# The second product's 256-column products moved into one column group, pieces of three thirds moved out of it

## The chip, the cores and the metric

The kernel runs on one core of a Trainium2 chip. The metric is the device time of one execution in microseconds. TensorE (PE in the profile) does the matrix products, VectorE (DVE), ScalarE (ACT) and GpSimd (POOL) the elementwise work, and SyncE (SP) and POOL issue the transfers. Matrix products are summed up in PSUM, which has eight banks of 512 float32 columns over 128 partitions.

## The reference

`x` is (8, 4096, 192), `weight` (8, 7), `w_in` (192, 2048), `w_out` (2048, 192), all float32.

```python
w = softmax(weight, axis=-1)                       # 7 taps for each of 8 heads
attn = causal depthwise convolution of x over the sequence with w
x = attn.reshape(32768, 192)
h = x @ w_in                                       # 32768 x 2048
g = h * np.clip(h + 3.0, 0.0, 6.0) / 6.0
return (g @ w_out).astype(np.float32)              # 32768 x 192
```

## The kernel before, in words

The 32768 tokens are worked on in 32 blocks of 1024. A block has a first layer (convolution, the product with `w_in`, and the hardswish) and a second layer (the product with `w_out`). Block 0 has a second layer of its own (`out_direct`), blocks 1 to 30 use the steady form of `second_layer`, and block 31 a variant of it for the end (`last`). This text is about the 30 steady blocks.

**First layer** (`first_layer`, matmuls on L512). Sixteen units go through four pairs of PSUM banks. When a unit's products are done, ACT applies a relu (L303), DVE multiplies (the gate, L307), and the pair of banks is free again. The second layer takes three of the four pairs for its banks `x_`, `b`, `y_`, `c`, `a`, and its two banks `f` and `h` are the fourth pair, `free_slots[0]`, which is the one that the last unit of the first layer has used.

**Second layer** (`second_layer`). The product with `w_out` is done by Strassen-like formulas: seven products, numbered 1 to 7, of sums of quarters of g and of w_out, each 96 output columns wide (three thirds of 32). The output of PE is cut into four column groups of 32, numbered 0 to 3 here, which write the PSUM partitions 0-31, 32-63, 64-95 and 96-127 (`first`, `second`, `third`, `fourth`). The groups work at the same time, so that four products of 32 output columns go on side by side. All of their matmuls are recorded on one line, L640.

A *plain* product of one third takes eight matmuls of 512 columns, two slots each (`plain`, `put(j, 2, ...)`). Products 1, 2, 4 and 5 have one third that is done by a second level of the same formulas: seven small products of four matmuls of 256 columns, one slot each (`small`, `level_two`), between which ACT copies intermediate results from one place of PSUM to another (`steps`: small product 1 goes to A, A is copied to B, 6 is added to B, B is copied to C, and so on). A float32 matmul runs as two passes.

The order is written out by hand. Each of the four groups has its own list and a clock in slots, and every list must end at 80. All other work of the stage (ACT copies, DVE sums, transfers, stores) is put in with `do(t, fn)`, at slot t - 0.5. At the end all events are sorted by slot and issued in that order, so that each engine gets its instructions in the order of those times. There is no planner, and no wait is written by hand: the framework puts in a semaphore wait where an instruction touches what an earlier one on another engine still uses.

```python
        def do(t, fn, *args, **kw):
            streams[3].append((t - 0.5, lambda: fn(*args, **kw)))
...
        events = sorted(((t, fn) for st in streams for t, fn in st), key=lambda x: x[0])
```

Before, product 2's small products are spread over the groups: 1, 7, 2 and 4 in group 0, 5 in group 1, 3 in group 2, 6 in group 3, with copies between them at fixed slots (20, 31.9, 39.6, 40, 44, 64, 64.4). The level two of product 1 is in group 1, of 4 in group 2 and of 5 in group 3. Group 0 has 16 matmuls of 256 columns, the others 32 each.

Of the kernel before, what the change touches and what calls it, by code (L numbers as in the profile page):

```python
# [25 lines left out]
def kernel(  # L26
# [16 lines left out]
    N = 512  # L43
    G = 2
    TB = G * N
    D2 = P // 2
# [41 lines left out]
    for base, dma in ((0, nc.scalar), (D2, nc.sync)):  # L88
        dma.dma_start(
            out=w_sb[base : base + D2],  # L90
            in_=weight.unsqueeze(1).to_broadcast([H, GJ, KC]),
# [126 lines left out]
    for n in range(AHEAD):  # L218
# [8 lines left out]
        out=e_sb[:], in0=w_sb[:], in1=mx[:].to_broadcast([P, KC]), op=ALU.subtract  # L227
# [54 lines left out]
    def take():  # L282
        return free_banks.pop(0)
# [72 lines left out]
    every = range(NP)  # L356
# [90 lines left out]
    def rows(q):  # L447
        return slice(q * QS, (q + 1) * QS)
# [9 lines left out]
    def add(out, x, y, op=ALU.add):  # L458
        nc.vector.tensor_tensor(out=out, in0=x, in1=y, op=op)  # L459
# [112 lines left out]
    halves = slice(0, TH), slice(TH, N)  # L572

    def four_parts(x):
        return [x[:, c::2, t] for t in halves for c in range(2)]
# [14 lines left out]
    def quarters(w):  # L590
        return [
            w_out[:, c::2, w, q * QS : (q + 1) * QS] for c in range(2) for q in range(2)
        ]
# [12 lines left out]
    def second_layer(i, between):  # L606
        last = i + 1 == NB
        ours = [free_slots.pop(0) for _ in range(3)]
        x_, b, y_, c, a, _ = (psum[:, 2 * n + k] for n in ours for k in range(2))
# [3 lines left out]
        copy = nc.scalar.copy  # L613
        m = slice(0, DH)
        lo, hi = halves
        both = nc.sync, nc.scalar
        first, second, third, fourth = (rows(q) for q in range(4))
        f, h = (psum[:, 2 * free_slots[0] + k] for k in range(2))
        end = h
        V = a[fourth]  # L620
        chains = {
            j: [bank[rows(j), t] for bank in (x_, y_) for t in halves] for j in (1, 2, 3)
        }
        A2, E2, C2, D2 = f[first, lo], f[second, hi], h[first, lo], h[third, hi]
        B2 = h[second if last else fourth, hi]
        j1 = 3 if last else 1
        late = {}

# [3 lines left out]
        def put(j, cost, fn):  # L632
            streams[j].append((clock[j], fn))
            clock[j] += cost

        def do(t, fn, *args, **kw):
            streams[3].append((t - 0.5, lambda: fn(*args, **kw)))

        def matmul(j, out, w, x, start):
            nc.tensor.matmul(  # L640
                out=out, lhsT=w, rhs=x, start=start, stop=True,
                tile_position=(0, j * QS), skip_group_check=True,
            )

        def plain(j, bank, n, q, chunks, start=False):
            x, w = prod[n]
            x = S3 if x is None else x
            for k, ch in enumerate(chunks):
                put(j, 2, lambda ch=ch, k=k: matmul(
                    j, bank[rows(j)], w_out[:, ch, w, q * QS : (q + 1) * QS], x[:, ch],  # L650
                    start and k == 0,
                ))
# [8 lines left out]
        def small(n, m_, out, start=False, j=3):  # L661

            x, w = prod[n]
            sums, ws = {
                1: (shared, w_s[:, 0]), 5: (s5, w_s[:, 1]), 2: (sums2, w_s[:, 2]),
                4: (sums4[0], w_s[:, 3]),
            }[n]
            x11, x12, x21, x22 = four_parts(x)
            z1, z2, z3, z4 = four_parts(sums)
            b11, t3, b21, b22 = quarters(w)  # L670
            t1, t2, t4 = (ws[:, k] for k in range(3))
            xm, wm = {
                1: (x11, b11), 2: (x12, b21), 3: (z4, b22), 4: (x22, t4),
                5: (z1, t1), 6: (z2, t2), 7: (z3, t3),
            }[m_]
            for u in range(NP // 2):
                put(j, 1, lambda u=u: matmul(
                    j, out, wm[:, u], xm[:, u], start and u == 0
                ))
# [16 lines left out]
        def fold(p, m136):  # L696
            add(p[second, hi], p[second, hi], p[second, lo])
            add(p[second, lo], m136, p[second, lo])
# [11 lines left out]
        def p2(r, t):  # L710
            return late["p2"][r, t]

        def p3(q):
            if last:
                plain_by_halves(q, 3, q, 0)
                plain_by_halves(q, 3, q, 1)
            else:
                plain(q, b, 3, q, in_fours)
# [6 lines left out]
        p4 = Fourth()  # L725

        def level_two(n, p, order, j=3):
            A, E, B, C = chains[j]
            steps = {
                1: lambda: copy(out=B, in_=A),  # L730
                2: lambda: copy(out=p()[first, lo], in_=A),
                6: lambda: copy(out=C, in_=B),
                5: lambda: copy(out=p()[second, lo], in_=E),
                7: lambda: copy(out=p()[second, hi], in_=C),
                3: lambda: copy(out=p()[first, hi], in_=C),
            }
            to = {1: A, 2: A, 6: B, 5: E, 7: C, 3: B, 4: C}
            for k in order:
                small(n, k, to[k], k in (1, 5), j)
                if k != 4:  # L740
                    late_by = {(1, 2): 8.1, (4, 2): 8.2 if last else 19.3}.get((n, k), 0.02 if n == 4 else 0)
                    do(clock[j] + late_by, steps[k])

        rest = 6, 2, 7, 5, 4, 3
        chunks, first_fill = list(every), [True]

        def fill(k):
            plain(3, a, 5, 2, [chunks.pop(0) for _ in range(k)], first_fill.pop() if first_fill else False)
# [2 lines left out]
            for ch in every[2:6]:  # L751
                by_half(3, (a, c)[t], 2, 2, ch, t)

        plain(0, b, 4, 2, every, True)
        small(2, 1, A2, True, 0)
        plain(0, c, 7, 0, every, True)
        small(2, 7, C2, False, 0)
        small(2, 2, A2, False, 0)
        plain(0, b, 6, 0, every)
        small(2, 4, C2, False, 0)  # L760
        p3(0)

        if last:
            plain(1, b, 1, 2, every, True)
            plain(1, c, 7, 1, every[:4], True)
            plain(1, a, 2, 2, every[:2], True)
            small(2, 6, B2, False, 1)
            plain(1, c, 7, 1, every[4:])
            small(2, 5, E2, True, 1)
            plain(1, b, 6, 1, every)  # L770
            plain(1, a, 2, 2, every[6:])
        else:
            level_two(1, lambda: p1, (1,), 1)
            plain(1, c, 7, 1, every[:4], True)
            level_two(1, lambda: p1, rest, 1)
            plain(1, c, 7, 1, every[4:])
            plain(1, b, 6, 1, every)
            small(2, 5, E2, True, 1)
        p3(1)

        level_two(4, lambda: p4, (1,), 2)
# [2 lines left out]
        level_two(4, lambda: p4, rest, 2)  # L784
        plain(2, c, 7, 2, every[ahead:])
        plain(2, b, 6, 2, every)
        small(2, 3, D2, False, 2)
        p3(2)

        if last:  # L790
            level_two(1, lambda: p1, (1,))
            fill(2)
            level_two(1, lambda: p1, rest)
            fill(4)
        else:
            plain(3, b, 1, 2, every, True)
            plain(3, c, 2, 2, every[:6], True)
            small(2, 6, B2, False)
            plain(3, c, 2, 2, every[6:])
            fill(4)  # L800
        level_two(5, lambda: late["p5"], (1,))
        fill(2)
        level_two(5, lambda: late["p5"], rest)
# [5 lines left out]
        assert clock == [80] * 4  # L809

        for t in halves:
            do(30 if t == hi else 29, copy, out=p4[third, t], in_=b[first, t])
        do(25.5, copy, out=p1[third], in_=b[second if last else fourth])
        do(20, copy, out=B2, in_=A2)
        do(31.9, copy, out=C2, in_=B2)
        do(39.6, copy, out=D2, in_=B2)
        do(40, lambda: copy(out=p2(second, hi), in_=C2))
        do(44, lambda: copy(out=p2(first, lo), in_=A2))
        do(44 if last else 64, lambda: copy(out=p2(second, lo), in_=E2))

        for t, job in between:
            do(t, job)
# [31 lines left out]
        if last:  # L854
            do(49, lambda: copy(out=late["p5"][third], in_=V))
        else:
            do(56.6, lambda: copy(out=p2(third, slice(0, N)), in_=c[fourth]))
        do(64.4, lambda: copy(out=p2(first, hi), in_=C2))
        if last:
            do(64.4, lambda: add(p2(third, slice(0, N)), a[second], p1[third]))  # L860
            for bank, t in ((a, lo), (c, hi)):
                do(64.4, lambda bank=bank, t=t: copy(out=bank[fourth, t], in_=p2(third, t)))
        do(64.4, lambda: fold(late["p2"], D2))
        whole = slice(0, 2 * QS if last else DH)
        do(64.6, lambda: add(late["p2"][whole], late["p2"][whole], p1[whole]))
        if last:
# [92 lines left out]
    with tc.manual_schedule():  # L959
# [4 lines left out]
            out=c_sb[:], in0=e_sb[:], in1=sm[:].to_broadcast([P, KC]), op=ALU.mult  # L964
# [14 lines left out]
        b = take()  # L979
        for cols in (N, N, N // 2):  # L980

            nc.tensor.matmul(  # L982
                out=psum[:, b, 0:cols], lhsT=zeros[:, 0:P], rhs=zeros[:, 0:cols],
# [59 lines left out]
        n = 3  # L1043
        for slot, (c, group) in enumerate(parts):
            first = slot < len(early)
# [27 lines left out]
        late = ctx.enter_context(tc.tile_pool(name="late", bufs=1, reuse_waits="tile"))  # L1073
# [60 lines left out]
        last = ctx.enter_context(tc.tile_pool(name="last", bufs=1, reuse_waits="tile"))  # L1134
# [55 lines left out]
```

## Time and profile before

| | |
|---|---|
| median of 3 runs | 2195.59 us (2195.41 to 2196.65) |
| the profiled execution's own time | 2195.6 us |
| its span | 2193.8 us |
| PE busy | 2188.3 us |
| DVE busy | 1953.5 us |
| ACT busy | 1230.1 us |
| POOL busy | 1178.8 us |
| matmuls of the second layer on `g` with `w_out` (L640) | 5960 of 512 and 256 columns, mean 503 ns |
| granted TensorE clock | 1.000 |

Busy time is the time in which an engine has at least one instruction at work; matmuls of different column groups overlap, so PE counts once for up to four. "PEld" is the load of weights into PE, which goes on beside matmuls. A row of the timeline gives the start in us, how long, the engine, the line, the operation, output and input tile, their shapes, and in square brackets the idle time before it and who ended it. The chain is read backwards from the last instruction; its shares say which engine's work set the time.

### The profile page before, as it was taken

The page shows a single profiled execution, that of the slowest core. Times are in us where ns is not written, and L with a number is a line of the kernel's source. Part 1 is how long each engine was busy: PE and PEld are TensorE (multiplying, and loading weights), DVE is VectorE, ACT ScalarE, POOL GpSimd, SP SyncE. Part 2 cuts the span into 40 slices and gives each one's busy share as a digit, 9 for nine tenths or more (in the row PEclk, how much of TensorE's full clock was granted, in tenths as well). Part 3 has the DMA queues.
Part 4 walks back from the last instruction along what each step waited for, and adds up shares of the span by engine and source line. Part 5 has one row for each costly group of instructions (what it writes and reads, how often), then busy time and mean ns, then how long its engine had stood idle before and what let it go on. Part 6 is the DMA issues. An engine that isn't in the chain of part 4 may idle for free.

```text
span 2193.8 us, 53991 instructions
## 1 busy us (share of the span) xinstructions
PE 2188.3 (100%) x22984; PEld 1501.9 (68%) x22984; DVE 1953.5 (89%) x1956; ACT 1230.1 (56%) x1800; POOL 1178.8 (54%) x1028
## 2 busy tenths in 40 slices
PE   9999999999999999999999999999999999999999
PEld 4467776677766677766777667776667776677766
DVE  8888998898998889988899888999888998899977
ACT  7355565554555655555546555455565555554654
POOL 2456654565544666445655456554456554565544
PEclk9999999999999999999999999999999999999999
DMA  6277778777778777797777878777877778777776
GB/s 159 60 138 146 147 147 151 141 146 145 148 139 157 141 139 146 147 159 131 147 147 145 148 145 145 145 146 145 159 135 139 147 148 154 135 147 144 135 143 112
DMA packets 352434, 312.59 MB, mean 142 GB/s; under 512 B 211904, under 2 KB 264640, under 8 KB 352192
## 3 DMA queue, kind: packets, MB, share of 16 engines
q0 software_dynamic: 114640, 233.87, 59.3%
q1 hardware_dynamic: 235624, 74.66, 16.9%
q8 instruction: 180, 2.95, 0.6%
q10 hardware_dynamic: 1928, 0.59, 0.1%
q14 instruction: 62, 0.51, 0.1%
HBM read 31.72 MB, written 25.17 MB: 26 GB/s over the span
## 4 chain that ended last, share of the span: by engine, by line
PE 100%; DVE 0%; issue 0%
PE psum L640 49%; PE psum L512 46%; PE psum L297 2%; PE psum L342 2%; PE psum L974 0%; PE psum L982 0%; PE psum L895 0%; DVE zeros L111 0%; DVE shared L922 0%; DVE x L96 0%; DVE half L233 0%; DVE bias_e L150 0%; DVE bias_e L149 0%
## 5 line engine op out<-in xcount | busy, mean ns | idle before, releaser
L640 PE MATMUL psum<-g,w_out 128*32 128x512 f32 (+1 forms) x5960 | 922.8, 503 | 0.0
L303 ACT ACTIVATE g<-psum,half 128x1024 f32<-128x1024 f32 (+1 forms) x528 | 574.4, 1092 | 485.6 <-PE psum L512 485.6
L307 DVE SCALAR_TENSOR_TENSOR g<-g,psum 128x1024 f32<-128x1024 f32 (+1 forms) x528 | 608.2, 1180 | 106.4 <-ACT g L303 106.1
L640 PE MATMUL psum<-s,w_out 128*32 128x512 f32 (+1 forms) x3024 | 657.9, 585 | 0.0
L640 PEld LDWEIGHTS psum<-g,w_out 128*32 128x32 f32 x5960 | 375.0, 110 | 248.9 <-issue 116.0
L512 PE MATMUL psum<-y_own,w_in 64*128 64x512 f32 x4464 | 515.1, 388 | 0.0
L512 PE MATMUL psum<-y_other,w_in 64*128 64x512 f32 x4464 | 510.9, 386 | 0.0
L512 PEld LDWEIGHTS psum<-y_own,w_in 64*128 64x128 f32 x4464 | 415.8, 184 | 112.1 <-issue 26.0
L512 PEld LDWEIGHTS psum<-y_other,w_in 64*128 64x128 f32 x4464 | 418.1, 184 | 87.8
L588 POOL TENSOR_TENSOR shared<-g,shared 128x256 f32<-128x256 f32 x248 | 358.0, 1444 | 54.8 <-DVE g L307 29.0
L1080 DVE SCALAR_TENSOR_TENSOR y<-x,c_sb,y 128x1536 f32<-128x1536 f32 x186 | 334.7, 1799 | 0.2
L554 POOL DMA_DIRECT2D s<-g x123 | 147.1, 1198 | 266.4 <-PE psum L640 123.5
L640 PE MATMUL psum<-g,w_s 128*32 128x256 f32 x1488 | 282.3, 379 | 0.0
L640 PEld LDWEIGHTS psum<-s,w_out 128*32 128x32 f32 x3024 | 197.2, 110 | 74.0 <-issue 16.0
L554 POOL DMA_DIRECT2D g<-g x124 | 180.8, 1519 | 106.7 <-DVE s L415 106.7
L640 PE MATMUL psum<-z,w_s 128*32 128x256 f32 x992 | 228.1, 379 | 0.0
L640 PE MATMUL psum<-z,w_out 128*32 128x256 f32 x992 | 227.2, 379 | 0.0
L459 DVE TENSOR_TENSOR g<-g 128x1024 f32<-128x1024 f32 x124 | 148.7, 1220 | 44.5 <-PE psum L640 44.5
L588 POOL TENSOR_TENSOR shared<-g 128x256 f32<-128x256 f32 x124 | 92.0, 742 | 171.4 <-DVE g L307 171.4
L640 PEld LDWEIGHTS psum<-g,w_s 128*32 128x32 f32 x1488 | 138.0, 110 | 42.7
L266 POOL DMA_DIRECT2D y_other<-y_own x90 | 48.0, 534 | 213.2 <-DVE shared L459 213.1
L554 POOL DMA_DIRECT2D z<-g x62 | 95.8, 1545 | 116.3 <-ACT z L557 116.3
(118 smaller groups left out, 2706.4 us busy)
## 6 DMA issues: line engine op xcount, KB each, us to landing
y_other<-y_own POOLq DMA_DIRECT2D x180, 384.0 KB, 8.1
g<-g POOLq DMA_DIRECT2D x124, 512.0 KB, 6.0
s<-g POOLq DMA_DIRECT2D x123, 512.0 KB, 6.4
z<-g POOLq DMA_DIRECT2D x62, 512.0 KB, 7.2
out_dram<-shared SPq DMA_DIRECT2D x376, 64.0 KB, 3.9
x<-in_x_dram SPq DMA_DIRECT2D x53, 388.5 KB, 5.7
z<-g SPq DMA_DIRECT2D x31, 512.0 KB, 3.3
stage<-in_moe_w_in_dram SPq DMA_DIRECT2D x16, 192.0 KB, 5.0
```

What stands on the lines that cost most here:

```text
L266: dma.dma_start(out=to[D2:P], in_=part[0:D2])
L297: nc.tensor.matmul(out=psum[:, b], lhsT=w[r], rhs=src, start=start, stop=stop, skip_group_check=onto,)
L303: nc.scalar.activation(r6, h, ACT.Relu, bias=half[:], scale=1.0 / 6.0)
L307: nc.vector.scalar_tensor_tensor(out=g_, in0=g_, scalar=1.0, in1=h, op0=ALU.min, op1=ALU.mult)
L342: lambda p=p: nc.tensor.matmul(out=bank[j * QS : (j + 1) * QS, tokens], lhsT=w_out[:, p, w, cols], rhs=x[:, p, tokens], start=(first and p ...
L459: nc.vector.tensor_tensor(out=out, in0=x, in1=y, op=op)
L512: nc.tensor.matmul(out=psum[:, 2 * slots[n] + k], lhsT=r32(w_in_parts[part][r, c, s]), rhs=r32(y_other[0][r, part, s] if group else y_own[ ...
L554: nc.gpsimd.dma_start(out=out, in_=x, accum_op=ALU.add)
L588: engine.tensor_tensor(out=o, in0=p, in1=q, op=op)
L640: nc.tensor.matmul(out=out, lhsT=w, rhs=x, start=start, stop=True, tile_position=(0, j * QS), skip_group_check=True,)
L1080: jobs.append(lambda k=k: nc.vector.scalar_tensor_tensor(out=y[:], in0=x[:, :, k : k + N], scalar=c_sb[:, k : k + 1], in1=y[:], op0=ALU.mu ...
```

## The change

It changes steady blocks alone (`last` keeps the old order).

- All seven small products of product 2 are now in group 0, through `level_two(2, ..., 0)`, with the places A, E in bank `f` and B, C in bank `h`, partitions `first`. Small product 1 moves from slot 16 to slot 4, right behind the first two chunks of plain product 4.
- The other six chunks of that plain third of product 4 go to group 3 (slots 16 to 28, into `a[fourth]`). What group 0 has summed up so far is copied there by ACT: `a[fourth] <- b[first]`, due at 4.2. `p4[third]` is then read from `a[fourth]`.
- Two chunks of the plain third of product 5 go from group 3 to group 1 (slots 60 to 64, into `a[second]`): ACT copies `a[second] <- a[fourth]` at 52.1 and back at 64.5.
- The last two chunks of the plain third of product 2 go from group 3 to group 2 (slots 60 to 64, into `a[third]`): ACT copies `a[third] <- c[fourth]` at 48.1, and `p2[third]` is read from `a[third]` at 64.4.
- The seven copies that joined product 2's scattered small products are gone. Each group now has 28 matmuls of 256 columns. The number of matmuls is the same.

In the changed kernel the second layer's matmuls are on L641, the six copies of level two on L731 to L736, the relu and the gate still on L303 and L307.

```diff
+        chains[0] = [bank[first, t] for bank in (f, h) for t in halves]
...
+                        (1, 2): 8.1, (4, 2): 8.2 if last else 19.3, (2, 2): 8, (2, 7): -0.05, (2, 5): 4,
...
-        plain(0, b, 4, 2, every, True)
-        small(2, 1, A2, True, 0)
-        plain(0, c, 7, 0, every, True)
-        small(2, 7, C2, False, 0)
-        small(2, 2, A2, False, 0)
-        plain(0, b, 6, 0, every)
-        small(2, 4, C2, False, 0)
...
+        else:
+            plain(0, b, 4, 2, every[:2], True)
+            level_two(2, lambda: late["p2"], (1,), 0)
+            plain(0, c, 7, 0, every, True)
+            level_two(2, lambda: late["p2"], rest[:5], 0)
+            plain(0, b, 6, 0, every)
+            level_two(2, lambda: late["p2"], rest[5:], 0)
         p3(0)
...
-            small(2, 5, E2, True, 1)
+            plain(1, a, 5, 2, every[4:6])
...
-        small(2, 3, D2, False, 2)
...
+            plain(2, a, 2, 2, every[6:])
...
             plain(3, b, 1, 2, every, True)
+            plain(3, a, 4, 2, every[2:])
             plain(3, c, 2, 2, every[:6], True)
-            small(2, 6, B2, False)
-            plain(3, c, 2, 2, every[6:])
-            fill(4)
+            fill(2)
+            chunks[2:4] = []
...
+            do(4.2, copy, out=a[fourth], in_=b[first])
+            do(48.1, copy, out=a[third], in_=c[fourth])
+            do(52.1, copy, out=a[second], in_=a[fourth])
+            do(64.5, copy, out=a[fourth], in_=a[second])
...
-            do(56.6, lambda: copy(out=p2(third, slice(0, N)), in_=c[fourth]))
+            do(64.4, lambda: copy(out=p2(third, slice(0, N)), in_=a[third]))
```

More of the change, by code (lines that the diff above doesn't have):

```diff
@@ L623, in second_layer @@
         }
+        chains[0] = [bank[first, t] for bank in (f, h) for t in halves]
         A2, E2, C2, D2 = f[first, lo], f[second, hi], h[first, lo], h[third, hi]
-        B2 = h[second if last else fourth, hi]
+        B2 = h[second, hi]
         j1 = 3 if last else 1
@@ L740, in level_two @@
                 if k != 4:
-                    late_by = {(1, 2): 8.1, (4, 2): 8.2 if last else 19.3}.get((n, k), 0.02 if n == 4 else 0)
+                    late_by = {
+                        (1, 2): 8.1, (4, 2): 8.2 if last else 19.3, (2, 2): 8, (2, 7): -0.05, (2, 5): 4,
+                    }.get((n, k), 0.02 if n == 4 else 0)
                     do(clock[j] + late_by, steps[k])
@@ L752, in last_third @@
                 by_half(3, (a, c)[t], 2, 2, ch, t)
-        plain(0, b, 4, 2, every, True)
-        small(2, 1, A2, True, 0)
-        plain(0, c, 7, 0, every, True)
-        small(2, 7, C2, False, 0)
-        small(2, 2, A2, False, 0)
-        plain(0, b, 6, 0, every)
-        small(2, 4, C2, False, 0)
+        if last:
+            plain(0, b, 4, 2, every, True)
+            small(2, 1, A2, True, 0)
+            plain(0, c, 7, 0, every, True)
+            small(2, 7, C2, False, 0)
+            small(2, 2, A2, False, 0)
+            plain(0, b, 6, 0, every)
+            small(2, 4, C2, False, 0)
+        else:
+            plain(0, b, 4, 2, every[:2], True)
+            level_two(2, lambda: late["p2"], (1,), 0)
+            plain(0, c, 7, 0, every, True)
+            level_two(2, lambda: late["p2"], rest[:5], 0)
+            plain(0, b, 6, 0, every)
+            level_two(2, lambda: late["p2"], rest[5:], 0)
         p3(0)
@@ L786, in second_layer @@
         plain(2, b, 6, 2, every)
-        small(2, 3, D2, False, 2)
+        if last:
+            small(2, 3, D2, False, 2)
+        else:
+            plain(2, a, 2, 2, every[6:])
         p3(2)
@@ L811, in second_layer @@
         for t in halves:
-            do(30 if t == hi else 29, copy, out=p4[third, t], in_=b[first, t])
+            do(30 if t == hi else 29, copy, out=p4[third, t], in_=(b[first, t] if last else a[fourth, t]))
         do(25.5, copy, out=p1[third], in_=b[second if last else fourth])
[L814 to L819, printed above, removed]
+        if last:
+            do(20, copy, out=B2, in_=A2)
+            do(31.9, copy, out=C2, in_=B2)
+            do(39.6, copy, out=D2, in_=B2)
+            do(40, lambda: copy(out=p2(second, hi), in_=C2))
+            do(44, lambda: copy(out=p2(first, lo), in_=A2))
+            do(44, lambda: copy(out=p2(second, lo), in_=E2))
+        else:
+            do(4.2, copy, out=a[fourth], in_=b[first])
+            do(48.1, copy, out=a[third], in_=c[fourth])
+            do(52.1, copy, out=a[second], in_=a[fourth])
+            do(64.5, copy, out=a[fourth], in_=a[second])
         for t, job in between:
@@ L856, in second_layer @@
         else:
-            do(56.6, lambda: copy(out=p2(third, slice(0, N)), in_=c[fourth]))
-        do(64.4, lambda: copy(out=p2(first, hi), in_=C2))
+            do(64.4, lambda: copy(out=p2(third, slice(0, N)), in_=a[third]))
+        if last:
+            do(64.4, lambda: copy(out=p2(first, hi), in_=C2))
         if last:
@@ L862, in second_layer @@
                 do(64.4, lambda bank=bank, t=t: copy(out=bank[fourth, t], in_=p2(third, t)))
-        do(64.4, lambda: fold(late["p2"], D2))
+        do(64.4, lambda: fold(late["p2"], D2 if last else chains[0][2]))
         whole = slice(0, 2 * QS if last else DH)
```

## The prediction

> **What bounds the kernel now.** I read the page's busy shares first, then the chain that ended last in order of time, then one steady block of the timeline, engine by engine, and last the compiled program of the changed kernel, which says what each matmul waits for.
>
> ```profile
> PE 2188.3 (100%) x22984; PEld 1501.9 (68%) x22984; DVE 1953.5 (89%) x1956; ACT 1230.1 (56%) x1800; POOL 1178.8 (54%) x1028
> ...
> PE 100%; DVE 0%; issue 0%
> PE psum L640 49%; PE psum L512 46%; PE psum L297 2%; PE psum L342 2%; PE psum L974 0%; PE psum L982 0%; PE psum L895 0%; DVE zeros L111 0%; DVE shared L922 0%; DVE x L96 0%; DVE half L233 0%; DVE bias_e L150 0%; DVE bias_e L149 0%
> ```
>
> What matters here is the 100% of PE, and that the chain never leaves it.
>
> ```profile
> 468.53 34.55 PE psum L640 x291
> 503.08 32.86 PE psum L512 x288
> ```
>
> PE never stands still: a steady block is 34.55 us of second layer (L640, the stage that the change edits) and 32.86 us of first layer (L512), and the 30 steady blocks repeat these two numbers. Asked who PE waits for from 99 us to 2190 us, the trace names nobody. So only two things can move the time: the number and length of the passes in the longest column group, and a wait that PE does not have today. In the stage that starts at 468.46 these rows carry the prices:
>
> ```profile
> 467.69 0.84 PE L512 MATMUL psum<-y_other,w_in 64*128 64x512 f32 x6
> 468.46 2.33 PE L640 MATMUL psum<-g,w_out 128*32 128x512 f32 x25
> 470.22 0.59 PE L640 MATMUL psum<-s,w_out 128*32 128x512 f32 x1
> ...
> 490.84 0.38 PE L640 MATMUL psum<-g,w_s 128*32 128x256 f32 x1
> ...
> 491.49 0.38 PE L640 MATMUL psum<-g,w_s 128*32 128x256 f32 x1
> ```
>
> ```profile
> 468.57 1.11 ACT L303 ACTIVATE g<-psum,half 128x1024 f32<-128x1024 f32 x1 [0.92 <-PE psum L512]
> 470.49 0.71 ACT L730 COPY psum<-psum 32x256 f32<-32x256 f32 x2 [0.80 <-PE psum L640]
> 475.63 0.71 ACT L732 COPY psum<-psum 32x256 f32<-32x256 f32 x2 [4.44 <-PE psum L640]
> ...
> 489.46 0.34 ACT L730 COPY psum<-psum 32x256 f32<-32x256 f32 x1 [0.65 <-PE psum L640]
> 489.74 1.48 ACT L477 ACTIVATE y_own<-y 128x1536 fp32r<-128x1536 f32 x1
> ```
>
> ```profile
> 469.72 1.22 DVE L307 SCALAR_TENSOR_TENSOR g<-g,psum 128x1024 f32<-128x1024 f32 x1 [0.81 <-ACT g L303]
> ```
>
> The reader is to see three places in time. Slot 4 of the 80 (a slot is a 256-column product, 0.43 us) is 470.22. The gate of the first layer's last unit, which reads the bank pair f, h, ends only at 469.72 + 1.22 = 470.94. ACT's first copies of the stage end at 470.49 + 0.71 = 471.20.
>
> **The change part by part.** *Passes.* Each product is two passes. Long passes follow each other every 0.43 us (plain products of one group start at 470.63, 471.06, 471.49), short ones every (491.49 - 490.84)/3 = 0.217 us. Groups 1 to 3 go from 24 long and 32 short products to 26 and 28, that is from 48 x 0.43 + 64 x 0.217 = 34.53 us to 52 x 0.43 + 56 x 0.217 = 34.51 us. Group 0 grows from 16 shorts to 28, to the same sum. So evening out saves 0.02 us a block, 30 x 0.02 = 0.6 us. I take it, bounds 0 and 1.2 us.
>
> *The first wait, at slot 4.* Before, group 0 first writes bank f at slot 16, about 468.46 + 16 x 0.432 = 475.4, long after the gate. Now it writes f at slot 4, and the compiled program has that short product waiting for DVE. Behind it on PE, in order, stand the slot-4 products of the other groups, so all four stop from 470.22 to 470.94. Worse, group 3's slot-4 product, into bank b, now waits for ACT: the new copy `a[fourth] <- b[first]` (due at 4.2) reads bank b, and the program keeps the two apart although they use different rows. On ACT that copy stands behind the two L730 copies that end at 471.20. Its own form, 32x512 from PSUM to PSUM, is not in the trace; a 32x512 copy out of PSUM takes 0.58 us (L637, L857), a 96x512 copy into PSUM 0.57 us, and a 32x256 copy between banks 0.34 against 0.36 us to SBUF. I take 0.57, with 0.34 (a 256-wide one) and 0.58 as ends. It runs from 471.22 to 471.79. From a release to the next engine's start is 0.04 us (ACT ends at 469.68, DVE starts at 469.72), and the first pass after a pause is longer by its unhidden weight load:
>
> ```profile
> L640 PE MATMUL psum<-g,w_out x192: 379/592/617, 468.5 to 502.5; 128*32 128x512 f32 x112, 128*32 128x256 f32 x80
> ...
> L297 PE MATMUL psum<-y_swapped,w_in x9: 589/589/693, 16.5 to 20.0; 64*128 64x512 f32 x9
> ```
>
> 617 - 592 = 0.025 us with a 32-column load, 693 - 589 = 0.104 us with a 128-column one; I take 0.03, since the load is a 32-column one here. Group 3 goes on at 471.86, so it loses 471.86 - 470.22 = 1.64 us (1.40 to 1.75). The gate's 0.72 us lies inside this and is not added. The stage ends with its latest group, and that is group 3.
>
> *The second wait, at slot 48.* Two long products before 490.84 put slot 48 at 490.84 - 4 x 0.43 = 489.12. There group 3 now adds to a[fourth], and a copy due at 48.1, `a[third] <- c[fourth]`, writes the same bank. The program has this product wait for that copy as well. On ACT it stands behind level two's first copy (L730 at 489.46, which waits for products ending at slot 48), before which nothing can start it: 489.46 + 0.34, then 0.57 from 489.82 to 490.39, then 0.07, against 489.12: 1.34 us. Part of the 0.34 us from slot to copy is the other groups' slower retirement, and after the first wait group 3 is itself the last; with 0.2 us for that it is 1.20. I take 1.27 (1.05 to 1.45).
>
> *Other waits.* At slots 20, 28 and 44 PE already depends on ACT copies. The pair L732 ends at 476.34, slot 20 is 477.10, so 0.76 us are spare. Group 3 running up to 1.64 - 0.72 = 0.9 us behind groups 1 and 2 can delay the release of those copies by as much, but it costs only the groups that are ahead. I take 0, up to 0.2 us a block.
>
> *ACT, DVE, POOL, SP.* ACT loses seven copies of 0.34 to 0.36 us (2.45 us) and gains six of them and four of 0.57 us (4.4 us), net 1.95 us a block. It is busy 20.57 of the stage's 34.55 us, and most new copies fall in its gaps (4.44 us idle before 475.63, 3.07 us before the last L735), so this costs nothing but for the two above; without that cover it would be 1.95 us. Counts and order of instructions on DVE, POOL and SP, their DMAs among them, are unchanged: whatever they issue moves with PE, and no transfer gets less time than before.
>
> *Sum.* 1.64 + 1.27 - 0.02 = 2.89 us a block, and the stage goes from 34.55 to about 37.4 us. 30 x 2.89 = 86.7 us. The profiled execution took 2195.6 us (span 2193.8 and 1.8 around it), the median is 2195.59, so the sum stands on either: 2282 us.
>
> *A rule beside it.* The conflict over banks is the program's. The Trainium skill, page "PSUM — Partial Sum Buffer", section "PSUM bank collisions raise a hardware error", says that two engines may use one bank at the same time if they are in different 32-partition quadrants. By that rule neither the copy out of b[first] nor the one into a[third] would have to hold group 3, and the sum would be the second rival's below; no run here shows it, and the compiled waits speak against it.
>
> **The rivals.** *It does what it says* (no new wait reaches PE): 2195.6 - 0.6 = 2195 us. For it speaks that no PE wait is in the trace now; against it that the gate ends 0.72 us after slot 4 whatever else happens. *Only the gate holds PE*, because group 3's two waits are met early: 0.72 + 0.07 = 0.79 us a block, 30 x 0.77 = 23 us, 2219 us. Against it: the copies stand in order behind copies that the trace shows ending at 471.20 and 489.80. *More than these two*: the waits at 20, 28 and 44 become real and the desynchronized groups retire each copy's source later, 0.6 us more a block: 2300 us. *The other side*: the groups' unevenness costs more than the pass counts say. The stage's 34.55 us against 80 slots of long passes only, 80 x 0.43 = 34.4, leaves at most 0.15 us a block, 4.5 us in all: 2191 us. It decides only if f were free at 470.22 and bank b at the same time; the row at 469.72 says no.
>
> **How the numbers follow.** Forecast 0.80; more waits 0.07; gate alone 0.06; does what it says 0.04; other side 0.03. The forecast's own bounds are (1.40 + 1.05) x 30 = 73 us and (1.75 + 1.45 + 0.2) x 30 = 102 us, 2269 to 2298. With the rival above at 2300, the range 2266 to 2301 leaves out little more than the three lower cases, 13 in 100, and some of the forecast's tail. About 0.2% (4.4 us) is what a measurement of this kernel can tell from no change: faster 0.03, same 0.04, slower 0.93.
>
> **What would show it.** In the changed kernel L641, the line of the second layer's matmuls, should take about 37.4 us a block, first layer 32.86 as before; PE should show two idle stretches, some 1.6 us after the stage's first 1.8 us (first released by DVE, then by ACT) and some 1.2 us near 22.5 us into it (by ACT); the new 32x512 copies should take 0.57 us. I am wrong if PE waits only for DVE, if the stage is near 34.5 us, or if a third place near slots 20 to 44 costs more than 0.2 us.

## The result and the profile after

The changed kernel takes 2281.24 us (median of 5 runs, 2280.97 to 2281.58), the one before 2195.92 us (5 runs): a ratio of 1.0388, 95% interval 1.0373 to 1.0403, slower. The forecast was 2282 us, within 2266 to 2301.

The first lines of the page of the changed kernel and its chain, to be held against the 100% and the unbroken chain of before:

```profile
span 2279.6 us, 54111 instructions
## 1 busy us (share of the span) xinstructions
PE 2239.5 (98%) x22984; PEld 1500.2 (66%) x22984; DVE 1955.7 (86%) x1956; ACT 1288.2 (57%) x1890; POOL 1177.0 (52%) x1028
...
PE 92%; ACT 5%; DVE 2%; issue 1%; ACTq 0%
```

PE has as many passes as before (22984), but the chain now leaves it, for ACT and DVE. Who PE waits for between 99 us and the end, where the same question had no answer before (columns: us in total, times, longest):

```profile
PE psum L641 <- ACT psum L638: 16.9, 30, 0.6
PE psum L641 <- DVE g L307: 14.0, 23, 0.6
PE psum L641 <- DVE x L81: 4.3, 7, 0.6
```

There are thirty waits for ACT and thirty (23 + 7) for the gate, one of each per steady block: L81 is a memset that ends within 0.01 us of the gate on L307, so the last two rows are one wait. L638 is the line of the copies. The list counts only the time in which no column group had a matmul at work. So what a block loses is larger, and group 3's wait for the first copy, during which the other groups still worked, is not in the list; it is read from the rows of the block below. One steady block in the chain in order of time (start, us, what):

```profile
484.44 1.22 DVE g L307
485.66 0.03 DVE s L415
485.69 0.02 issue
485.71 17.68 PE psum L641 x158
503.39 0.03 issue
503.42 0.36 ACT shared L732
503.78 0.96 ACT s L557
504.74 0.02 issue
504.76 0.36 ACT shared L734
505.12 0.58 issue
505.70 0.06 ACT psum L731
505.77 0.29 issue
506.06 0.56 ACT psum L638
506.62 0.04 issue
506.67 13.98 PE psum L641 x82
```

The same block on PE and on ACT:

```profile
483.18 1.93 PE L641 MATMUL psum<-g,w_out 128*32 128x512 f32 x24
485.71 0.40 PE L641 MATMUL psum<-g,w_out 128*32 128x256 f32 x1 [0.61 <-DVE x L81]
...
486.54 0.62 PE L641 MATMUL psum<-g,w_out 128*32 128x512 f32 x2
...
506.67 1.93 PE L641 MATMUL psum<-g,w_out 128*32 128x512 f32 x16 [0.56 <-ACT psum L638]
```

```profile
485.20 0.71 ACT L731 COPY psum<-psum 32x256 f32<-32x256 f32 x2 [0.80 <-PE psum L641]
485.94 0.55 ACT L638 COPY psum<-psum 32x512 f32<-32x512 f32 x1
...
505.70 0.34 ACT L731 COPY psum<-psum 32x256 f32<-32x256 f32 x1 [0.58 <-issue]
506.06 0.56 ACT L638 COPY psum<-psum 32x512 f32<-32x512 f32 x1
```

The stage starts at 483.18, so slot 4 is at 483.18 + 1.76 = 484.94 (470.22 - 468.46 before). The gate ends at 485.66 and group 0's small product starts at 485.71. The new copy ends at 485.94 + 0.55 = 486.49, and group 3 goes on at 486.54, 1.60 us late. Its 44 slots to slot 48 (by the starts of the passes, 40 slots in 20 long products of some 0.859 us, 4 in short ones of 0.432 us) end at 505.44, and it goes on at 506.67, 0.05 us after the copy's end: 1.23 us late. Between 505.51 and 506.67 no group starts a pass, though only group 3 waits for the copy.

Ahead of the second copy the chain runs through ACT's earlier work (L732, L557, L734). That work is not what held the copy: ACT then stood idle for 0.58 us, until L731 started at 505.70. L731 copies the result of group 3's small product that ends at slot 48, and it starts 0.26 us after 505.44. The profile names no releaser for it here; for the same copy in the kernel before it names PE (the row at 489.46).

The stage grows from 34.55 us to 37.40 us in the mean of the steady blocks, from the first matmul to the first one of the next stage; the span grows by 2279.6 - 2193.8 = 85.8 us, 2.86 us for each of the 30 blocks. Only part of this shows as idle time of PE, whose busy time grew by 2239.5 - 2188.3 = 51.2 us with the same passes: while one group waits, PE still counts as busy as long as another works.

### The profile page after: what moved, and what is told of

Its sections match the earlier page's. It is cut to its first block, busy times and chain, and to the rows that moved or that the text cites. A ratio compares the mean times of both kernels' runs of the same rounds, so it can differ in the third digit from the quotient of the medians.

```text
span 2279.6 us, 54111 instructions
## 1 busy us (share of the span) xinstructions
PE 2239.5 (98%) x22984; PEld 1500.2 (66%) x22984; DVE 1955.7 (86%) x1956; ACT 1288.2 (57%) x1890; POOL 1177.0 (52%) x1028
## 4 chain that ended last, share of the span: by engine, by line
PE 92%; ACT 5%; DVE 2%; issue 1%; ACTq 0%
PE psum L512 45%; PE psum L641 43%; PE psum L297 2%; PE psum L342 2%; DVE g L307 2%; ACT g L303 1%; ACT s L557 1%; ACT psum L638 1%; ACT shared L732 0%; ACT shared L734 0%; PE psum L995 0%; PE psum L1003 0%; ACT psum L731 0%; PE psum L916 0%; DVE zeros L111 0%
## 5 line engine op out<-in xcount | busy, mean ns | idle before, releaser
L641 PE MATMUL psum<-g,w_out 128*32 128x512 f32 (+1 forms) x5960 | 1013.9, 505 | 35.1 <-ACT psum L638 16.9
L303 ACT ACTIVATE g<-psum,half 128x1024 f32<-128x1024 f32 (+1 forms) x528 | 574.2, 1092 | 488.0 <-PE psum L512 472.3
L307 DVE SCALAR_TENSOR_TENSOR g<-g,psum 128x1024 f32<-128x1024 f32 (+1 forms) x528 | 608.1, 1180 | 108.9 <-ACT g L303 108.7
L641 PEld LDWEIGHTS psum<-g,w_out 128*32 128x32 f32 x5960 | 382.9, 109 | 366.5 <-issue 86.5
L641 PE MATMUL psum<-s,w_out 128*32 128x512 f32 (+1 forms) x3024 | 616.8, 587 | 0.0
L641 PE MATMUL psum<-g,w_s 128*32 128x256 f32 x1488 | 286.9, 380 | 0.0
L641 PEld LDWEIGHTS psum<-g,w_s 128*32 128x32 f32 x1488 | 135.0, 109 | 95.1 <-issue 9.6
L641 PE MATMUL psum<-z,w_out 128*32 128x256 f32 x992 | 185.8, 380 | 0.0
L641 PE MATMUL psum<-z,w_s 128*32 128x256 f32 x992 | 185.6, 379 | 0.0
L641 PEld LDWEIGHTS psum<-s,w_out 128*32 128x32 f32 x3024 | 144.9, 108 | 10.2 <-issue 0.5
```

What stands on the lines that cost most here:

```text
L303: nc.scalar.activation(r6, h, ACT.Relu, bias=half[:], scale=1.0 / 6.0)
L307: nc.vector.scalar_tensor_tensor(out=g_, in0=g_, scalar=1.0, in1=h, op0=ALU.min, op1=ALU.mult)
L641: nc.tensor.matmul(out=out, lhsT=w, rhs=x, start=start, stop=True, tile_position=(0, j * QS), skip_group_check=True,)
```

## The experiments

Three theories were set against each other. A: two waits in column group 3, one for the copy out of bank b and one for the copy into bank a, whose size is set by what stands ahead of the copy on ACT; the gate's wait lies inside the first. B: ACT's 1.95 us of additional copies in a block delay the stage wherever they are put. C: the two waits at slot 4, for the gate and for the copy, add up.

**copy52: the second wait taken away.** The copy is put behind group 3's two long products of slots 48 to 52.

```diff
-            do(48.1, copy, out=a[third], in_=c[fourth])
+            do(52.05, copy, out=a[third], in_=c[fourth])
```

> The changed kernel with the copy a[third] <- c[fourth] at 52.05 in place of 48.1, behind group 3's product at slots 48 to 52. Theory A (two waits in group 3): the second wait goes, 506.67 - 505.44 = 1.23 us a block, first wait stays: 2281 - 37 = 2244 us. Rival B (the 1.95 us more of ACT work a block is what delays the stage, wherever it is put): 2281 us.

Measured 2245.86 us (before 2195.58; ratio 1.0229, 1.0212 to 1.0246). The wait for ACT is gone from the list of PE's waits:

```profile
PE psum L641 <- DVE g L307: 14.0, 23, 0.6
PE psum L641 <- DVE x L81: 4.3, 7, 0.6
```

By the kernels' times the second wait is worth (2281.24 - 2245.86)/30 = 1.18 us a block and the first one alone (2245.86 - 2195.58)/30 = 1.68 us. These times also hold small differences outside the stage (the first layer takes 32.90 us here, 32.88 in the changed kernel and 32.86 before). The stage itself takes 36.17 us, so the second wait is 37.40 - 36.17 = 1.23 us and the first one 36.17 - 34.55 = 1.62 us. B falls: the copy is still there.

**bank_y: the same copy out of a bank that no matmul writes then.**

```diff
-            plain(0, b, 4, 2, every[:2], True)
+            plain(0, y_, 4, 2, every[:2], True)
...
-            do(4.2, copy, out=a[fourth], in_=b[first])
+            do(4.2, copy, out=a[fourth], in_=y_[first])
```

> The changed kernel with group 0's first two chunks in y_[first] in place of b[first], and the copy at 4.2 from there: same copies, same times, another bank. Theory A: group 3 no longer waits for ACT at slot 4, all groups wait for the gate alone, 485.71 - 484.94 = 0.77 in place of 1.60 us: 2281 - 30 x 0.83 = 2256 us, and PE is released there by DVE only. Rival B: 2281 us.

Measured 2261.46 us (ratio 1.0300, 1.0285 to 1.0316), 5 us above A's figure, 20 us below the changed kernel. A block of its chain:

```profile
481.08 1.22 DVE g L307
482.30 0.03 DVE s L415
482.34 0.02 issue
482.36 17.26 PE psum L641 x161
```

At slot 4 PE is now released by the gate and runs on to the second wait. So group 3's wait for ACT came from sharing bank b and not from the data: rows 0-31 were read, rows 96-127 written. Most of the 5 us are in the second wait: all groups are in step here, and it costs 0.15 us a block more than behind the first one (bank_y_gate8).

**gate8: bank f first written at slot 8.**

```diff
+            plain(0, c, 7, 0, every[:2], True)
             level_two(2, lambda: late["p2"], (1,), 0)
-            plain(0, c, 7, 0, every, True)
+            plain(0, c, 7, 0, every[2:])
```

> The changed kernel with two chunks of plain product 7 ahead of small product 1 in group 0, so that bank f is first written at slot 8, after the gate's end. Theory A (the gate's wait lies inside the one for ACT): no change, 2281 us within 3. Rival C (the two waits at slot 4 add up): 2281 - 30 x 0.77 = 2258 us.

Measured 2282.08 us (ratio 1.0394, 1.0379 to 1.0410). The gate is gone from the list of PE's waits, and the time is the same, as A says. C falls. Without the gate both waits for ACT are in the list, sixty in all:

```profile
PE psum L641 <- ACT psum L638: 39.8, 60, 0.8
```

**before_copy: the first wait put into the kernel before.**

```diff
         do(20, copy, out=B2, in_=A2)
+        if not last:
+            do(4.2, copy, out=a[fourth], in_=b[first])
```

> The kernel before with one copy more, a[fourth] <- b[first] at 4.2; nothing uses what it writes (a[fourth] is started anew at slot 36). Theory A: this alone brings the first wait, but of all four groups' slot-4 products, 1.60 us a block: 2196 + 48 = 2244 us. Rival B: 0.55 us of ACT work in a gap of 4.4 us: 2196 us, at most 2196 + 17 = 2213.

Measured 2245.2 us (ratio 1.0226, 1.0211 to 1.0241), 49.6 us or 1.65 us a block more for one copy of 0.56 us in a gap, without any other part of the change. This shows the price of waiting for such a copy there, and not what made the wait: group 0's own matmul at slot 4 adds to the very rows of b that the copy reads, so that it would have to wait by its data too, and as the first of slot 4 it holds up the other three groups. In a block's chain the copy releases the whole rest of the stage:

```profile
479.83 0.56 ACT psum L637
480.39 0.04 issue
480.44 32.90 PE psum L640 x274
513.34 7.70 PE psum L512 x65
```

**first_on_act: the copy ahead of the two others on ACT.**

```diff
-            do(4.2, copy, out=a[fourth], in_=b[first])
+            do(3.99, copy, out=a[fourth], in_=b[first])
```

> The changed kernel with the copy a[fourth] <- b[first] due at 3.99 in place of 4.2, so that it stands ahead of the two L731 copies on ACT. Theory A (the queue ahead of the copy on ACT is part of the first wait): it ends at 485.20 + 0.55 = 485.75 in place of 486.49, group 3 loses 0.86 in place of 1.60 us: 2281 - 22 = 2259 us. If the copy itself were the whole price: 2281 us.

Measured 2262.24 us (ratio 1.0303, 1.0289 to 1.0317), 19 us less than the changed kernel, where 22 were expected. In the changed kernel's block the first wait's 1.60 us are 0.26 until ACT's first copy starts, 0.74 for the two copies ahead, 0.55 for the copy itself and 0.05 to the release. This run takes out the 0.74. The 3 us that it fell short of the expectation are about what the second wait takes back (0.15 us a block), since the groups are again nearly in step: the gate holds them for 0.77 us, the copy group 3 for 0.83. That is also why the time is nearly bank_y's.

**bank_y_gate8: only the second wait left.** Both edits from above.

> The changed kernel with first chunks in y_[first] and small product 1 at slot 8, the copy still at 48.1. Theory A: only the second wait is left, 1.23 us a block: 2196 + 30 x 1.21 = 2232 us. Rival C (waits at slot 4 add up, then gate8 would have gained and this gains the sum 0.77 + 1.60): 2281 - 71 = 2210 us.

Measured 2237.32 us (before 2195.77; ratio 1.0188, 1.0174 to 1.0202): 41.6 us, 1.38 us a block, 5 us more than expected.

```profile
497.34 0.06 ACT psum L731
497.40 0.29 issue
497.69 0.56 ACT psum L638
498.26 0.04 issue
498.30 13.98 PE psum L641 x82
```

The same links as in the changed kernel, but the wait is 1.38 us when all groups come to slot 48 in step and 1.23 us behind the first wait. The expectation had taken the size from the changed kernel. The difference stands ahead of the copies: this block's stage starts at 476.29, group 3's slot 48 comes 22 x 0.859 + 4 x 0.432 = 20.63 us later, at 496.92, and L731 starts 0.42 us after it, against 0.26 us in the changed kernel, where group 3 alone is late. With it bank_y adds up: (2261.46 - 2195.58)/30 = 2.20 us, 1.38 of it here and about 0.8 at the gate.

**all3: none of the waits, everything else of the change.** All three edits.

> The changed kernel with all three edits (copy at 52.05, first chunks in y_[first], small product 1 at slot 8). All copies of the change are kept. Theory A: no wait of PE is left, only the evened counts: 2196 - 0.5 us, that is 2195 to 2196.5 us. Rival B (ACT's extra work): 2281 us. If further waits at slots 20, 28 or 44 count: 2200 us or more, with PE idle there.

Measured 2197.06 us (before 2195.77; ratio 1.0006, 0.9997 to 1.0015), 0.6 us above the range expected. All copies are kept, ACT is busier by 61 us than before, and the chain is PE's alone again:

```profile
PE 2189.7 (100%) x22984; PEld 1487.6 (68%) x22984; DVE 1952.7 (89%) x1956; ACT 1291.2 (59%) x1890; POOL 1178.8 (54%) x1028
...
PE 100%; DVE 0%; issue 0%
```

```profile
401.71 34.54 PE psum L641 x274
436.25 32.91 PE psum L512 x288
```

So without the waits the change is worth nothing that can be measured: 34.54 for 34.55 us in the second layer. No version here beats the kernel before.

All runs beside each other; the stage is the second layer's, in the mean of the 30 steady blocks of the trace, from its first matmul to the first one behind it:

| kernel | waits left | time, us | stage, us |
|---|---|---|---|
| before | none | 2195.6 to 2195.9 | 34.55 |
| changed | gate, first copy, second copy | 2281.24 | 37.40 |
| copy52 | gate, first copy | 2245.86 | 36.17 |
| bank_y | gate, second copy | 2261.46 | 36.74 |
| gate8 | first copy, second copy | 2282.08 | 37.40 |
| before_copy | first copy | 2245.20 | 36.20 |
| first_on_act | gate, first copy (shorter), second copy | 2262.24 | 36.75 |
| bank_y_gate8 | second copy | 2237.32 | 35.92 |
| all3 | none | 2197.06 | 34.54 |

## Why the prediction was right

*The passes.* The forecast put the evening out at 0.02 us a block. all3 shows the stage at 34.541 us against 34.551 in the mean of the blocks: 0.01 us. The size is at the edge of what rows printed to 0.01 us can give; it is right that it is nothing.

*The first wait.* 1.64 us forecast, 1.60 read from the block, 1.62 by the stage of copy52. The steps hold one by one: the gate lies inside (gate8), the program keeps ACT and PE apart by bank and not by rows (bank_y), and the queue of two copies ahead is 0.74 us of it (first_on_act). The 32x512 copy between banks takes 0.55 to 0.56 us, where 0.57 was taken. The release takes 0.05 us, where 0.07 was taken with the weight load.

*The second wait.* 1.27 us forecast, between 1.34 for groups in step and 1.20 for group 3 as the last one. By the runs it is 1.38 us in step and 1.23 us behind the first wait. The two cases and their order were right, and the changed kernel is the second of them. The 0.2 us from slot to copy behind the 1.20 were not worked out from a row, and 1.27 was the middle of the two cases; that they came so near (the row shows 0.26 us) is in part luck. That the bank alone makes this wait was not tried by itself, as bank_y did for the first one; it is inferred from the kernel's text, by which the copy writes rows 64-95 of bank a and the matmul rows 96-127.

The sum forecast was 1.64 + 1.27 - 0.02 = 2.89 us a block; the stage grew by 37.40 - 34.55 = 2.85 us.

*The signs.* One did not come as it was put: PE was to show idle stretches of some 1.6 and 1.2 us. It stands idle for 0.61 and 0.56 us: at slot 4 the other groups go on once the gate has ended, and at slot 48 they are still at work when group 3 stops. The lengths forecast are those of group 3's waits. The places and the engines are as forecast, DVE and then ACT at slot 4 and ACT at slot 48.

*The other waits* at slots 20, 28 and 44 were taken as 0. PE's list of waits names none of them, but it would not show a wait of one group alone. That group 3 lost nothing there follows from the block: counted without any wait from 486.54 it is at slot 48 at 505.44, and the copy of what it has done by then starts 0.26 us later. *ACT's extra copies* were taken as hidden but for the two; all3 shows that. DVE and POOL have the instruction counts that they had (1956 and 1028), and of their work the chain of a block holds only the gate and 0.03 us of the sum behind it.

*The rivals.* Bank_y is what "only the gate holds PE" says of slot 4, and there it is true once the bank is not shared. "More than these two" and "the other side" are not seen: there is no third wait, and without the waits the stage takes 34.54 us. The Trainium skill's rule that was set beside the rivals (page "PSUM — Partial Sum Buffer", section "PSUM bank collisions raise a hardware error") lets two engines use one bank at the same time in different 32-partition quadrants. This program waits all the same: the matmul into rows 96-127 went on at 486.54, 0.05 us after the copy of rows 0-31 had ended. Whether the chip would have needed that wait was not tried.

## What to carry to other kernels

Where PE works without a pause, look first at what each moved instruction shares with other engines. Here every group had 80 slots before and after; trading four short products for two long ones in three of the groups gave 0.01 us, and one copy of 0.55 us out of a bank that another group was writing took 1.62 us (copy52). In an order written out by hand, a copy's slot says when it is queued; when it ends follows from what stands ahead of it on its engine and from when its source is released, and the compiled program's waits say who stands behind it. A wait of one column group stops the others too: at the second wait no group started a pass for 1.15 us. The order in which PE's instructions are issued fits this: the other groups' next matmuls stand behind the waiting one.

## What the runs showed that was not expected

Two waits in one group cost less together than apart: 1.62 us (copy52) and 1.38 us (bank_y_gate8) are 3.00 us, and together they are 2.85 us. The second is smaller when its group is already the last.

In all3 the first layer's stage takes 32.91 us where it took 32.86 us before, with the same instructions. That is 1.3 us in the whole kernel, about the difference of the medians and within the interval. Even groups alone do not bring it, since bank_y_gate8, which has them too, shows 32.87 us, while copy52 shows 32.90 us; its cause stays open.
